# A transformer-block kernel with batched block-sorted attention: v mixed one batch ahead, loads reordered, matmuls in hand-set order

## The chip, the cores and the metric

The kernel runs on one core of one Trainium2 chip. The metric is the device time in microseconds (us) of one execution; lower is better. The engines are TensorE (PE), VectorE (DVE), ScalarE (ACT), GpSimd (POOL) and SyncE (SP, which here only issues transfers). Medians and 95% intervals are given. A run over 1.5% above the fastest of its kernel is called slow and is left out of every ratio.

A ratio is the mean time of one kernel's fast runs over the mean of the other's fast runs of the same rounds on the same chip. It is therefore not quite the ratio of the two medians that stand beside it.

## The reference

```python
# q, k, v: (4, 8, 768, 64); 8 blocks of 96 rows; w_tok (768,768), w_ch1 (512,2048), w_ch2 (2048,512)
P = sort_net                                  # (4, 8, 8, 8)
for _ in range(5):
    P = softmax over the last axis, then normalised over the one before it
k_sorted = einsum('bhij,bhjcd->bhicd', P, k_b)   # every block becomes a mix of 8 blocks
v_sorted = einsum('bhij,bhjcd->bhicd', P, v_b)
attn = softmax(scale * q_b @ k_sorted^T)         # inside each block of 96
x = (attn @ v_sorted), heads joined              # (4, 768, 512)
# then, per batch:
u   = x + lam * (w_tok @ (alpha1 * x + beta1))   # token mixing
out = u + lam * (relu((alpha2 * u + beta2) @ w_ch1) @ w_ch2)   # MLP over channels
```

Everything is held to a tolerance that the kernel meets with 16-bit operands.

## The kernel before

Each batch goes through: mixing v and k with P on TensorE, scores, exponentials on ACT, the value product, token mixing, and the two MLP matmuls ("hidden", tile `h_ps`, and "output", tile `ch_ps`). The MLP of batch b-1 is interleaved with the attention of batch b, so that TensorE always has wide matmuls to run while attention's small ones wait for ACT and DVE. ("Spins" are dummy matmuls, tile `spin_ps`, that the program runs early on while TensorE has nothing else.)

GpSimd issues the loads of q, k and v of the next batch (software queue). SP issues, in the order of its program, everything else (hardware queue; in r12 below the turns of q take SP from 79.05 to 88.43, and the next store is issued at 88.53): the turning of q (`qT<-qn`) and of the MLP input (`a2T<-u`) by DMA transposes, the stores, and the *regrouping* of mixed v, which goes out to memory (`vscr<-vA`) and comes back in another layout (`Vs<-vscr`, packets of 128 bytes).

```python
def load_raw(b, kv):                 # v or k of a batch, two transfers of 384 KB (batch 0 differs)
    ...
    for th in range(2):
        pool.dma_start(raw[th*64:(th+1)*64, :], src[b].rearrange(...)[th])

def cross_q(b):                      # q turned by six DMA transposes, issued by SP
    with tc.issue_after(regroup[b - 1].ins):
        for kt in range(NT):
            nc.sync.dma_start_transpose(qT_of[b][:, :, kt, :], ...)

def mix_v(b, banks=2, groups=range(6), copies=(...)):
    for n in groups[::banks]:
        vps = ...
        pe.matmul(vps[...], lhsT, raw[...], start=True, stop=True)
        copies[...](vA[...], vps[...])
    if groups[-1] < 5:
        return
    for th in range(2):              # regrouping: out ...
        nc.sync.dma_start(vscr[b, ...], vA[th*64:(th+1)*64, :, :])
    for par in range(2):             # ... and back
        regroup[b] = nc.sync.dma_start(Vs[b % NV][...], vscr[b]...)

def moe_ch(b, hf, kks=range(3)):     # output matmuls, residual, store
    ...
        ost = att.tile([128, C], FT, name="ost", tag="ost", bufs=2)
        ...
        dve.tensor_tensor(ost[:, lo:hi], cps[:], u_of[b][kt][:, lo:hi], ALU.add)
        nc.sync.dma_start(out[...], ost[0:96, lo:hi])

# ---- main order, from the end of batch 0's token mixing on (cut) ----
for n in range(6):
    moe_h(0, 0, range(5 + n, 6 + n))
    mix_v(1, 1, range(n, n + 1), (dve.tensor_copy,))
pool.tensor_copy(gate[:], Vs[1][0:1, 0, 0:2])   # the gate: GpSimd waits for batch 1's regrouped v
load_raw(2, 1)                                  # and only then loads v and k of batch 2
load_raw(2, 0)
...
pe.fixed = False                                # the scheduler orders the matmuls from here
for b in range(1, B):
    if b > 1:
        ...
        mixing_matrices(b)
        mix_v(b)                                # v of batch b mixed at the head of its own stage
        ...
        mix_k(b)
    emit_attention(b)
    ...                                         # MLP of batch b-1, token mixing of b
```

The *gate* is a tiny copy on GpSimd that reads the regrouped v of batch 1. Everything behind it in GpSimd's program, the loads of batch 2 above all, waits until that v has landed. `pe.fixed` says whether TensorE's instructions keep the program's order or the scheduler may move them.

The softmax here doesn't subtract the row's maximum and nothing guards it: scores larger than these inputs give would overflow.

## Time and profile before

| what | before |
|---|---|
| timed median of 3 runs | 269.09 us (268.78 to 269.38) |
| profiled span | 266.8 us |
| PE busy | 257.6 us, 97% |
| half clock on TensorE | none until the kernel's end |

The page of the kernel before, its first lines. The row of digits gives the busy tenths of PE in 40 equal slices; `PEclk` is the granted TensorE clock in tenths.

```profile
span 266.8 us, 5149 instructions
...
PE 257.6 (97%) x2049; PEld 141.6 (53%) x2059; DVE 154.8 (58%) x333; ACT 125.8 (47%) x232; POOL 92.5 (35%) x100
...
PE   7799999999999999999999999999999999999993
...
PEclk9999999999999999999999999999999999999999
...
PE 89%; ACT 4%; DVE 4%; issue 1%; DMA 1%; DVEq 0%; ACTq 0%
```

TensorE is the limit: it is never idle for a whole slice, and 89% of the chain that ended last is its own work. A gain has to come from TensorE's small gaps or from work taken off it.

The next lines are the timeline of PE in the kernel before: start, duration, engine, operation, tiles, count.

```profile
18.09 0.38 PE L65 MATMUL sc_ps<-qT,kT 64*96 64x96 f16 x8
...
42.64 2.60 PE L65 MATMUL h_ps<-a2T,W1p 128*128 128x384 bf16 x15
...
105.89 1.03 PE L65 MATMUL v_ps<-raw,bigV 128*128 128x512 f16 x4
107.59 0.59 PE L65 MATMUL v_ps<-raw,bigV 128*128 128x512 f16 x2
```

First scores start at 18.09, the first hidden matmul at 42.64, and v of batch 2 is mixed only at 105.89. GpSimd in the same kernel:

```profile
66.80 0.18 POOL L65 COPY gate<-Vs 1x2 f16<-1x2 f16 x1
66.92 1.08 POOL L65 DMA_DIRECT2D raw<-in_v_dram  x2
...
76.35 4.49 POOL L65 DMA_DIRECT2D qn<-in_q_dram  x5
```

The gate opens at 66.80 and v of batch 2 is issued at once, 39 us before TensorE wants it. Most of q comes after it. The next line is the view of the transfers of the kernel before, for those issued from 66 to 69 us: number, size of one, median us from issue to landing.

```profile
raw<-in_v_dram POOLq DMA_DIRECT2D x2, 384.0 KB, 8.4
```

So v of batch 2 lands near 76.

### The profile page before, as it was taken

What the parts mean: (1) busy time and instruction counts of PE and PEld (TensorE: products, weight loads), DVE (VectorE), ACT (ScalarE), POOL (GpSimd) and SP (SyncE); (2) the same over time, 40 slices, a digit from 0 to 9 for tenths busy, and PEclk for the clock granted to TensorE, in tenths of its full rate; (3) what the DMA queues carried; (4) which work ended last, traced back from release to release, by engine and by line L of the source; (5) the groups of instructions that cost most, each with busy time, mean ns of one, the idle gap of its engine ahead of it and who ended that gap; (6) DMA issues with size and microseconds to landing.
All of it is one profiled execution on the core that took longest, in us unless ns stands there. A gap on an engine that the chain in (4) does not pass through costs nothing.

```text
span 266.8 us, 5149 instructions
## 1 busy us (share of the span) xinstructions
PE 257.6 (97%) x2049; PEld 141.6 (53%) x2059; DVE 154.8 (58%) x333; ACT 125.8 (47%) x232; POOL 92.5 (35%) x100
## 2 busy tenths in 40 slices
PE   7799999999999999999999999999999999999993
PEld 2467745565565444554565444554565445545542
DVE  5878788629567966722585966704675962042033
ACT  3376757643585312980375404970474305504600
POOL 8524689203575615007917225002409000000000
PEclk9999999999999999999999999999999999999999
DMA  6999999999999544499996342494200432012012
GB/s 83 174 208 251 207 210 207 211 216 112 211 157 155 113 84 117 114 82 89 202 211 136 61 100 80 118 98 62 80 2 2 81 76 79 2 39 79 2 39 79
DMA packets 62423, 30.88 MB, mean 116 GB/s; under 512 B 48888, under 2 KB 58112, under 8 KB 62400
## 3 DMA queue, kind: packets, MB, share of 16 engines
q0 software_dynamic: 23024, 15.60, 39.4%
q1 hardware_dynamic: 39280, 14.89, 32.6%
q8 instruction: 16, 0.26, 0.4%
q14 instruction: 7, 0.06, 0.1%
q10 hardware_dynamic: 96, 0.07, 0.1%
HBM read 32.78 MB, written 8.65 MB: 155 GB/s over the span
## 4 chain that ended last, share of the span: by engine, by line
PE 89%; ACT 4%; DVE 4%; issue 1%; DMA 1%; DVEq 0%; ACTq 0%
PE ch_ps L65 31%; PE h_ps L65 30%; PE tok_ps L65 12%; PE x_ps L65 5%; PE sc_ps L65 4%; ACT kT L65 2%; PE v_ps L65 2%; PE k_ps L65 1%; PE q_ps L65 1%; ACT et L65 1%; DVE csum L65 1%; DVE P L65 1%; PE m_ps L65 1%; DVE rsum L65 1%; DMA P<-in_sort_net_dram 1%
## 5 line engine op out<-in xcount | busy, mean ns | idle before, releaser
L65 PE MATMUL h_ps<-a2T,W1p 128*128 128x384 bf16 x512 | 93.4, 326 | 0.1
L65 ACT ACTIVATE hTa<-h_ps 128x384 bf16<-128x384 f32 x96 | 45.9, 492 | 68.1 <-PE h_ps L65 67.0
L65 PE MATMUL ch_ps<-W2p,hTa 128*128 128x512 bf16 (+2 forms) x290 | 65.9, 370 | 0.5
L65 PEld LDWEIGHTS <-W1p 128*128 128x128 bf16 x512 | 47.5, 98 | 30.3 <-issue 0.9
L65 DVE TENSOR_TENSOR ch_ps<-ch_ps,lamB 128x512 f32<-128x512 f32 (+2 forms) x25 | 16.9, 676 | 63.2 <-PE ch_ps L65 60.5
L65 POOL TENSOR_SCALAR u<-b1lB,rs 128x512 f32<-128x512 f32 x18 | 28.8, 1610 | 64.1 <-DVE ost L65 59.3
L65 PEld LDWEIGHTS <-hTa 128*128 128x128 bf16 x300 | 28.7, 98 | 32.4
L65 PE MATMUL tok_ps<-x,w_tokT 128*128 128x512 f16 x144 | 32.1, 379 | 0.0
L65 POOL TENSOR_TENSOR u<-x,u 128x512 f32<-128x512 f16 x22 | 25.3, 1181 | 18.1 <-DVE x L65 17.3
L65 ACT ACTIVATE et<-sc_ps 96x768 f16<-96x768 f32 x32 | 24.9, 807 | 11.7 <-PE sc_ps L65 11.7
L65 ACT CAST u<-u 128x512 f16<-128x512 f32 x24 | 14.8, 618 | 24.8 <-DVE u L65 24.8
L65 PE MATMUL ch_ps<-W2p,hTb 128*128 128x512 bf16 (+2 forms) x100 | 25.0, 371 | 0.0
L65 PEld LDWEIGHTS <-w_tokT 128*128 128x128 f16 x180 | 14.8, 97 | 16.1
L65 DVE TENSOR_TENSOR tok_ps<-tok_ps,a1lB 128x512 f32<-128x512 f32 x24 | 16.5, 692 | 7.3 <-PE tok_ps L65 7.3
L65 DVE CAST kT<-k_ps 64x512 f16<-64x512 f32 x24 | 16.5, 688 | 3.4 <-PE k_ps L65 3.0
L65 DVE TENSOR_TENSOR x<-x_ps,recip 96x512 f16<-96x512 f32 (+2 forms) x32 | 17.6, 554 | 0.9
L65 DVE TENSOR_TENSOR u<-tok_ps,u 128x512 f32<-128x512 f32 x24 | 16.4, 688 | 1.7
L65 ACT ACTIVATE hTb<-h_ps 128x384 bf16<-128x384 f32 x32 | 15.3, 497 | 3.8 <-PE h_ps L65 3.4
L65 DVE TENSOR_TENSOR ost<-ch_ps,u 128x512 f32<-128x512 f32 (+2 forms) x25 | 16.6, 665 | 0.6
L65 POOL DMA_DIRECT2D qn<-in_q_dram x18 | 15.5, 875 | 4.2 <-PE q_ps L65 3.4
L65 PEld LDWEIGHTS <-hTb 128*128 128x128 bf16 x100 | 9.6, 98 | 10.9
L65 PEld LDWEIGHTS <-et 96*128 96x128 f16 (+2 forms) x288 | 12.4, 99 | 4.6 <-issue 1.2
(95 smaller groups left out, 214.7 us busy)
## 6 DMA issues: line engine op xcount, KB each, us to landing
out_dram<-ost SPq DMA_DIRECT2D x23, 192.0 KB, 2.2
raw<-in_v_dram POOLq DMA_DIRECT2D x8, 384.0 KB, 8.9
raw<-in_k_dram POOLq DMA_DIRECT2D x8, 384.0 KB, 10.9
vscr<-vA SPq DMA_DIRECT2D x6, 384.0 KB, 4.4
Vs<-vscr SPq DMA_DIRECT2D x6, 384.0 KB, 7.7
W1p<-in_moe_w_ch_dram POOLq DMA_DIRECT2D x4, 512.0 KB, 10.1
W2p<-in_moe_w_ch_dram POOLq DMA_DIRECT2D x4, 512.0 KB, 17.9
qn<-in_q_dram POOLq DMA_DIRECT2D x12, 128.0 KB, 5.8
```

The costliest lines, as they stand in the source:

```text
L65: ins = getattr(self.eng, name)(*args, **kwargs)
```

## The change

Intent: take switches between small and wide matmuls out of the attention stages, and start the first scores earlier. Its parts: (1) batch 0's k and v load by halves, k first; (2) the six copies that sort `w_tok` move from DVE to GpSimd; (3) v of batch 1 loads ahead of W1 and is mixed from the end of batch 0's attention on; W2 loads ahead of batch 2; (4) TensorE order is set by hand from batch 1 on: a `weave` of MLP matmuls with fewer, longer attention groups, and v of batch b+1 is mixed inside batch b's stage; (5) rows of u are made earlier, in 11 row buffers, from which results are stored directly (no `ost`).

```diff
@@ loads at the start @@
-    load_q(0)
-    load_raw(0, 1)
-    load_raw(0, 0)
+    load_q0(1)
+    load_raw0(0)          # k and v by halves, k first
+    load_raw0(1)
...
+    load_raw(1, 1)        # v of batch 1, ahead of W1
+    load_w1(range(2))
+    for n in range(3):
+        sort_wtok(n)      # now pool.tensor_copy
...
@@ end of batch 0 @@
+    mixes(1, 0)
     prep_rs()
...
+    load_q(1)
+    load_w2(range(4))     # all of W2 here: 40.8 us in the trace
+    tok_part(0, 0)
+    mixes(1, 1)
+    tok_part(0, 1)
+    mixes(1, 2)           # v of batch 1 regrouped from here on
...
@@ head of batch 1 @@
-    pool.tensor_copy(gate[:], Vs[1][0:1, 0, 0:2])
-    load_raw(2, 1)
-    load_raw(2, 0)
+    pool.tensor_copy(gate[32:64, :], Vs[1][32:64, 0, 0:2])
+    load_q(2)
+    load_raw(2, 1)
+    load_raw(2, 0)
+    cross_q(2, regroup[1])
+    moe_rows(1, range(5))
+    pe.fixed = True
@@ the loop over batches @@
-        if b > 1:
-            mixing_matrices(b)
-            mix_v(b)
-            mix_k(b)
-        emit_attention(b)
+        steps = ... attention_steps(b, ...)
+        if b < B - 1:
+            at = len(steps) - (3 if b == 1 else 6)
+            steps[at:at] = [(g, lambda n=n: mixes(b + 1, n)) for n, g in enumerate((1.2, 0.7, 1.1))]
+        weave(fill, steps)        # fill: MLP matmuls of batch b-1, in hand-set portions
+        run(fill)
@@ output @@
-            ost = att.tile([128, C], FT, name="ost", tag="ost", bufs=2)
+            u32 = u_of[(b, kt)]
-                nc.sync.dma_start(out[...], ost[0:96, lo:hi])
+                nc.sync.dma_start(out[...], u32[0:96, lo:hi])
```

(Cut to its core; names and lines are those of the change, arguments shortened where marked by dots.)

## The prediction

> **What bounds the kernel now.** TensorE. The page gives PE 257.6 us busy of a 266.8 us span (the timed median, 269.09, is 2.3 above the span), and the chain of waits is 89% PE. Busy time overcounts, so I took start-to-start times of matmuls from the timeline: 216 ns for 128x512, 162 for 128x384, about 30 for attention's small ones. The span then divides so (us):
> - 0 to 11.5: normalisation of the sort matrices, a DVE/ACT latency chain; PE only spins.
> - 11.5 to 34.0: batch 0's attention. Useful matmuls about 13.5, ten spins 2.2, nearly 7 of waits and switches. First scores at 18.1, because k loads last: its first half lands at 16.0 (issue plus landing time).
> - 34.0 to 42.6: token mixing, no gaps.
> - 42.6 to 262.4: gapless except 2.7 to 2.8 in each of three attention stages. There a change from wide matmuls to scores costs 0.12 and back 0.11, to k mixing 0.11; the rest is short waits.
> - End: 4.4 after the last matmul, unchanged.
>
> **What the change does, costed.**
> 1. Batch 0: k/v load by halves, k first; q turned during normalisation; ten spins out; uniform tail matmuls in the value product (mixed forms now cost about 0.09 a switch). First scores should come at about 14, and each head pair take about 2.9 of PE. Alone this would end the stage at about 28.5.
> 2. But w_tok lands at about 23 as before, and its sorting moves from DVE (six copies, 2.8 us) to GpSimd. [...] the trace shows only other operations there (1.2 and 1.6 us for 512). [...] v of batch 1, behind w_tok, lands at about 29.5. Row sums end at about 32 instead of 34.0: half of step 1's gain is eaten by arrivals.
> 3. v mixing of batch 1 (1.3 us of PE; ACT evicts at 1.0 each) moves in front of the first hidden matmul, which starts at about 41.4 instead of 42.6: gain about 2.5.
> 4. Attention of batches 1 to 3: eight attention groups instead of about fourteen, between hand-set stretches of MLP matmuls. [...] Gaps 2.7 to about 1.7 per batch: gain about 3.
> 5. Other matmul work is unchanged; DVE/ACT/GpSimd shifts are off the chain.
>
> Gain 5.5 to 6 in all.
>
> **Prediction.** 263.4 us, 8 in 10 between 260.0 and 267.5. Faster by over 2% (below 263.7): 0.52; within 2%: 0.45; slower: 0.03.
>
> **What would show it.** (1) first scores near 14; (2) PE waits for w_tok transposes between 24 and 31, released by GpSimd copies; (3) first hidden matmul at 40 to 43; (4) fewer, longer attention groups, gaps under 2 per batch; (5) last 47 us (MLP of batch 3) identical.
>
> **What would make it wrong.** GpSimd copies much quicker (then 261) or slower; loads of batch 2 colliding with W2 and the regrouping of batch 1's v: v of batch 2 is wanted near 71 and may land at 73 to 76, which in a fixed PE order stalls everything for 2 to 5; ACT, which takes more copies (gather, v mixing), falling behind between hidden-layer evictions and exponentials; the fixed order losing to the scheduler's.

The forecast's sum came to a span near 261 and a time of 263.4 us: a gain of 5.5 to 6, made of 2.5 for the first hidden matmul (point 3) and 3 for the gaps (point 4). The 32 for the row sums, and through it the 2.5 of point 3, contains the time of the sorting, as the author's estimate; the 3 of point 4 stands on the costs read from the trace.

## More of the kernel before

SP:

```profile
52.19 1.15 SPq L343 DMA_DIRECT2D vscr<-vA  x2
59.21 2.46 SPq L348 DMA_DIRECT2D Vs<-vscr  x2
...
83.10 7.17 SPq L149 DMA_TRANSPOSE qT<-qn  x5
90.37 8.90 SPq L601 DMA_TRANSPOSE a2T<-u  x6
...
109.26 1.10 SPq L343 DMA_DIRECT2D vscr<-vA  x2
```

SP never has two of these large jobs at one time: regrouping of batch 1 (52 to 61), turning of q (one transfer at 71, the other five from 83 to 90), turning of the MLP input (90 to 99), regrouping of batch 2 (from 109). That spacing looks like idle room. It is slack: time between a transfer's landing and its use.

## The result, and the profile after

| what | before (same chip) | after |
|---|---|---|
| timed median | 269.24 us (268.78 to 271.41), 4 runs | 280.00 us (278.65 to 281.05), 4 runs |
| ratio of the fast runs | | 1.038, 95% interval 1.031 to 1.046 |
| profiled span | 266.8 us | 276.9 us |
| half clock before the last 4 us | none | 13.65 us |

The change is slower by nearly 4%, where a gain of 2% was predicted. The page after:

```profile
span 276.9 us, 5127 instructions
...
PE 251.6 (91%) x2047; PEld 140.6 (51%) x2047; DVE 145.4 (53%) x317; ACT 136.2 (49%) x246; POOL 93.1 (34%) x100
...
PE   5988899999700999999999999999999999999994
...
PEclk9999999999965899999999999999999999999999
...
PE 76%; DMA 13%; POOL 6%; DVE 3%; issue 1%; ACT 1%; DVEq 0%; POOLq 0%
```

PE is busy 6 us less than before, yet the span is 10 longer. Two slices of the PE row read 0, and in the slices around them the granted clock falls. The whole loss is in one place. The timeline of PE after; the bracket gives the idle time just before the line and what ended it.

```profile
14.63 0.56 PE L65 MATMUL sc_ps<-qT,kT 64*96 64x96 f16 x16
...
42.34 2.88 PE L65 MATMUL h_ps<-a2T,W1p 128*128 128x384 bf16 x15
...
73.03 1.46 PE L65 MATMUL ch_ps<-W2p,hT 128*128 128x512 bf16 x6
89.84 1.01 PE L65 MATMUL v_ps<-raw,bigV 128*128 128x512 f16 x2 [15.35 <-DMA raw<-in_v_dram]
90.65 1.91 PE L65 MATMUL ch_ps<-W2p,hT 128*128 128x512 bf16 x4
```

The first scores come at 14.63 as predicted. Then TensorE stands still for 15.35 us because its next matmul in the fixed order mixes v of batch 2, and that v has not landed. The wait costs more than its own length: the windows on both sides of its end (length, then each engine's busy time, then PEclk, DMA share, GB/s) show a lower granted clock.

```profile
74.30:89.80 15.50, 0.19 (x1) 0.00 (x0) 0.50 (x2) 0.00 (x0) 7.73 (x5) 0.65 1.34 119
89.80:103.50 13.70, 13.66 (x98) 6.60 (x99) 6.99 (x15) 6.19 (x7) 1.56 (x1) 0.90 0.90 149
```

A mean of 0.90 over 13.7 us means 2.7 us at half clock after the restart, so about 1.4 us more. In that stretch the two v matmuls took 1.01 us where they take 0.59 at full clock. The clock record of this run shows half clock (0.50) for 13.65 us, from 78.9 to 92.5: it began about 4.4 us after TensorE had stopped, and ended 2.7 us after the restart. What sets its beginning and its length is not shown.

Why is v late? GpSimd after:

```profile
24.20 4.79 POOL L65 COPY wtp<-wt 128x1152 f16<-128x1152 f16 x6 [5.53 <-DMA wt<-in_moe_w_tok_dram]
...
40.78 2.99 POOL L65 DMA_DIRECT2D W2p<-in_moe_w_ch_dram  x4
66.30 0.18 POOL L65 COPY gate<-Vs 32x2 f16<-32x2 f16 x1 [22.53 <-DMA Vs<-vscr]
...
66.90 5.26 POOL L65 DMA_DIRECT2D qn<-in_q_dram  x6 [0.42 <-PE h_ps L65]
72.10 1.14 POOL L65 DMA_DIRECT2D raw<-in_v_dram  x2
```

and SP after:

```profile
47.61 11.32 SPq L364 DMA_DIRECT2D Vs<-vscr  x2
70.54 22.87 SPq L140 DMA_TRANSPOSE qT<-qn  x6
```

The view of the transfers after, for those issued from 72 to 73.2, and one line of the same view over the whole span, for all twelve DMA transposes of q:

```profile
raw<-in_v_dram POOLq DMA_DIRECT2D x2, 384.0 KB, 16.5
```

```profile
qT<-qn SPq DMA_TRANSPOSE x12, 8.3
```

Read together, three things push v of batch 2 from "landing near 76, wanted at 106" to "landing just before 89.8, wanted at 74".

1. The gate opens at 66.30, hardly earlier than before (66.80), although batch 1's v is mixed some 10 us earlier. (The two gates are not quite alike. The one before reads row 0, filled by the first of the two transfers that bring v back, and stood behind a load of q. The changed one reads rows 32 to 63, which need both. By the landing of the second transfer v is back at 66.15 instead of 68.42.) The regrouping reads back in 128-byte packets while W2 (issued at 40.78) arrives in 1 KB packets. In the records of the packets, the regrouping's queue and W2's move almost the same number of packets in each 2 us from 52 to 60: 386 and 385, 376 and 376, 382 and 381, 382 and 383. When W2 is in, regrouping alone moves 2,128 (62 to 64). What makes the counts equal is not shown. One record for one means an eighth of the bytes for the small ones: 0.05 MB in 2 us beside 0.38 MB of W2, where the regrouping alone moves 0.27 MB.
2. Behind the gate the six loads of q come first: 5.26 us of issue, and their 128-byte packets occupy the queue until about 75. v is issued at 72.10.
3. SP turns q meanwhile: of its 22.87 us it waits 11.8 for q to land, and its transposes fly beside the load of v. By the records of the packets, the loads of v and k together move 0.15 to 0.25 MB in each 2 us from 80 to 90; where almost nothing else flies (the kernel before, from 70 to 76) they move 0.35 to 0.37. Each suffers: the median turn takes 8.3 us to land, and v takes 16.5 us instead of 8.4.

### The profile page after: what moved, and what is told of

Read it like the earlier page. It is cut to its first block, busy times and chain, and to the rows that moved or that the text cites. A ratio compares the mean times of both kernels' runs of the same rounds, so it can differ in the third digit from the quotient of the medians.

```text
span 276.9 us, 5127 instructions
## 1 busy us (share of the span) xinstructions
PE 251.6 (91%) x2047; PEld 140.6 (51%) x2047; DVE 145.4 (53%) x317; ACT 136.2 (49%) x246; POOL 93.1 (34%) x100
## 4 chain that ended last, share of the span: by engine, by line
PE 76%; DMA 13%; POOL 6%; DVE 3%; issue 1%; ACT 1%; DVEq 0%; POOLq 0%
PE h_ps L65 29%; PE ch_ps L65 29%; PE tok_ps L65 9%; DMA wt<-in_moe_w_tok_dram 6%; DMA raw<-in_v_dram 6%; POOL qn L65 3%; PE sc_ps L65 2%; PE x_ps L65 2%; POOL wtp L65 2%; PE k_ps L65 1%; PE v_ps L65 1%; POOL raw L65 1%; DVE u L65 1%; PE q_ps L65 1%; DVE tok_ps L65 1%
## 5 line engine op out<-in xcount | busy, mean ns | idle before, releaser
L65 PE MATMUL h_ps<-a2T,W1p 128*128 128x384 bf16 x512 | 89.1, 326 | 0.1
L65 PE MATMUL ch_ps<-W2p,hT 128*128 128x512 bf16 (+2 forms) x400 | 88.4, 373 | 0.0
L65 ACT ACTIVATE hT<-h_ps 128x384 bf16<-128x384 f32 x128 | 60.4, 492 | 53.2 <-PE h_ps L65 52.7
L65 PEld LDWEIGHTS <-hT 128*128 128x128 bf16 x400 | 38.0, 99 | 42.1 <-issue 1.3
L65 DVE CAST kT<-k_ps 64x512 f16<-64x512 f32 x30 | 20.6, 687 | 3.9 <-PE k_ps L65 3.3
L65 DVE RECIPROCAL recip<-x_ps 96x8 f32<-96x8 f32 (+1 forms) x32 | 6.2, 195 | 27.5 <-PE x_ps L65 27.4
L65 ACT CAST vA<-v_ps 128x1024 f16<-128x1024 f32 x9 | 9.0, 1010 | 22.0 <-PE v_ps L65 22.0
L65 PE MATMUL v_ps<-raw,bigV 128*128 128x512 f16 x18 | 5.9, 410 | 15.3 <-DMA raw<-in_v_dram 15.3
L65 DVE TENSOR_TENSOR u<-ch_ps,u 128x512 f32<-128x512 f32 (+2 forms) x25 | 16.7, 667 | 0.8
L65 PEld LDWEIGHTS <-et 96*128 96x128 f16 (+1 forms) x288 | 12.0, 105 | 3.0 <-DVE x L65 0.6
```

The source lines that it names most:

```text
L65: ins = getattr(self.eng, name)(*args, **kwargs)
```

## The experiments

All kernels were built from the changed kernel ("after"). All outputs are right. Ratios are against the kernel before, on the same chip in the same rounds (medians of before lay from 268.58 to 269.24 us). "Wait" is the idle time of PE in the profile that names a transfer or an engine as its releaser.

| run | what it does | timed median, us | ratio (95%) | largest PE waits after 40 us |
|---|---|---|---|---|
| after | the change | 280.00 | 1.038 (1.031 to 1.046) | v of batch 2, 15.3 |
| e1_v_first | v, k ahead of q | 275.56 | 1.021 (1.014 to 1.028) | MLP input 3.7; 3.6 |
| e2_mix_after_tok | v mixed after token mixing | 283.27 | 1.050 (1.044 to 1.056) | row of u 8.7; 4.2; 2.8 |
| e3_no_gate | no gate | 272.72 | 1.013 (1.008 to 1.018) | MLP input 5.1; v 1.0 |
| e4_both | e1, v mixed at end of stage | 283.99 | 1.053 (1.045 to 1.062) | hidden 8.9; 4.7 |
| r5_defer_regroup | e1, regroup held back | 268.20 | 0.998 (0.995 to 1.001) | MLP input 3.6 |
| r6_all | r5, turning held, batch 3 gated | 275.08 | 1.024 (1.020 to 1.028) | v of batch 3, 9.4 |
| r8_defer_turn | only turning of q held back | 286.60 | 1.063 (1.057 to 1.069) | v of batch 3, 15.6; of 2, 6.1 |
| r9_cleared | r6, batch 3 loaded early | 269.94 | 1.005 (1.003 to 1.008) | regrouped v, 3.6 |
| r10_cleared_dve_sort | r9, sorts on DVE | 274.19 | 1.020 (1.018 to 1.021) | regrouped v, 4.7; (sort, 2.8) |
| r11_cleared_w2_gated | r9, W2 behind the gate | 271.66 | 1.010 (1.005 to 1.014) | 3.9; v of batch 2, 2.8 |
| r12_cleared2 | r5, batch 3 early, q of 3 gated | 272.27 | 1.010 (1.006 to 1.013) | row of u 6.1 |
| r14_rows12 | r12, 12 row buffers | 267.62 | 0.995 (0.991 to 1.000) | MLP input 3.2 |
| r15_split | write of v, turning, read | 264.68 | 0.983 (0.980 to 0.986) | MLP input, 1.4 at most |
| r16_split12 | r15, 12 row buffers | 265.43 | 0.986 (0.982 to 0.990) | 1.2 at most |

### First round: which part of the queue makes v late, and can it simply be wanted later?

**e1_v_first.** v and k of batch 2 go ahead of q.

```diff
-    load_q(2)
     load_raw(2, 1)
     load_raw(2, 0)
+    load_q(2)
     cross_q(2, regroup[1])
```

> Change with one edit: v and k of batch 2 are loaded ahead of q of batch 2 (all still behind the same gate). Theory (the loss is one wait of the fixed TensorE order for v of batch 2, which is late because q of batch 2 is loaded ahead of it): v lands about 10 us after its issue near 67, so at 76 to 78 instead of 89.7; the wait at its mixing (reached at 74) shrinks from 15.5 to 2 to 4 us, no half-clock stretch follows, time 264 to 267 us. Rival A (the hand-set order as such is slow, v is only where it shows): the wait moves elsewhere and the time stays above 274. Rival B (the gate alone makes it late): v still lands after 85, time above 274.

Measured: 275.56 us (272.09 to 277.05, one of four slow), ratio 1.021. The wait for v is gone:

```profile
74.73 0.59 PE L65 MATMUL v_ps<-raw,bigV 128*128 128x512 f16 x2
```

So the load order, with what flies beside it, is enough to remove the whole wait; the gate still opened at 66.08. But the gain expected did not come. (The profile is of the fastest run, with a mean clock of 0.991; the other three had 0.972 to 0.974, so they lost more to the lower clock than it shows.) New waits of 3.7 and 3.6 us stand before hidden matmuls, for the turned MLP input of batch 1 (released by DVE steps that themselves wait for the transposes). SP shows why:

```profile
93.26 2.56 SPq L364 DMA_DIRECT2D Vs<-vscr  x2
95.92 4.06 SPq L716 DMA_DIRECT2D out_dram<-u  x1
...
101.58 7.98 SPq L648 DMA_TRANSPOSE a2T<-u  x6
```

With v mixed on time, its regrouping (read back at 93.26) now runs ahead of the MLP-input transposes, and the stores behind it are held: the first takes 4.06 us to issue, and SP issues nothing else meanwhile. In the kernel before, v was mixed at 106, after the transposes (90 to 99).

**e2_mix_after_tok.** v of batch 2 is mixed after batch 1's token mixing, where the kernel before has it; loads unchanged.

```diff
-        if b < B - 1:
+        if 1 < b < B - 1:
             at = len(steps) - ...
...
+        if b == 1:
+            for n in range(3):
+                mixes(2, n)
         run(moe_ch(b - 1, 1, (1, 2)))
```

> Change with one edit: v of batch 2 is mixed after the token mixing of batch 1 (reached at about 96) instead of inside batch 1's attention (74); loads unchanged. Theory: v still lands near 90, nothing waits for it, the 15.5 us wait and about 1.5 us lost to the half clock behind it vanish: 260 us span, 261 to 263.5 timed, all other stages as in the change. Rival A (the fixed order is slow): other waits of over 5 us in total appear, time above 267.

Measured: 283.27 us, ratio 1.050: no faster than the change itself. Its profile fell on a slow run, so its waits are read for their places and releasers, not for a comparison of times. Token mixing waits 8.7 us for a row of u: GpSimd cannot make the row because its buffer is still being stored, and the stores stand behind the turning of q on SP (70.7 to 95.3). In the change as given the long wait for v hid that: the row came at 96.5 and token mixing began only at 105. A wait is not only cost; it also holds back everything behind it that would have collided.

**e3_no_gate.** The gate is dropped.

```diff
-    pool.tensor_copy(gate[32:64, :], Vs[1][32:64, 0, 0:2])
```

> Change without the gate that holds batch 2's loads until v of batch 1 is regrouped; order q, v, k kept. Theory (the wait for the gate, until 66.3, is the first half of v's lateness, q in front the second): v of batch 2 lands at 72 to 78; but the regrouping of v of batch 1 (128 B packets) now shares the DMA engines for longer and lands after 66, so a smaller wait at the first value product of batch 1 (reached at 67.3) appears. Time 264 to 270. Rival B (gate alone): time as without any wait, about 262. If the gate does not matter: above 274.

Measured: 272.72 us, ratio 1.013. q of batch 2 is issued at 59.06 and v at 64.26; the wait for v is 1.0 us at 76.37. So dropping the gate alone is worth about 7 us (ratio 1.013 against 1.038). Again the MLP input is late (5.1 us).

**e4_both.** e1 with v's mixing pushed to the end of the weave.

```diff
+            moved = steps[at:at + 3]
+            del steps[at:at + 3]
+            steps[at] = (1.9, steps[at][1])
+            steps += moved
```

> Change with v and k of batch 2 loaded ahead of q, and the three v mixings of batch 2 moved from the middle to the end of batch 1's attention weave (reached at about 81 instead of 74). Theory: v lands at 76 to 78, before it is wanted, no TensorE wait over 1 us after 43: 260 us span, 261 to 263 timed, about 2.5 to 3% under the kernel before. Rival A: above 267.

Measured: 283.99 us, ratio 1.053. The miss is large: hidden matmuls wait 4.7 us until 109.2 and 8.9 until 126.4. The view names ACT for the second, but behind ACT is DVE, which waits 12.0 us, until 122.0, for the last MLP-input transpose (issued at 107.92, landed at 121.89). The regrouping moved to 96, straight between the MLP-input transposes; the loads of batch 3 (issued 103 to 110) and the turning of its q (111 to 132) fly beside the last of them. Mixing v later is no repair while SP's order stays.

After this round the theory was: the lateness of v is one case of a more general thing. The new order has shortened the distance between every large transfer and its use, and SP's transfers now stand in the wrong order.

### Second round: the order on SP

**r5_defer_regroup.** e1, and the regrouping of v of batch 2 is held until the MLP-input transposes of batch 1 are issued.

```diff
-        if groups[-1] < 5:
+        if groups[-1] < 5 or b == 2:
             return
+        regroup_v(b)
...
         moe_a(b)
+        if b == 1:
+            with tc.issue_after(turned[-1].ins):
+                regroup_v(2)
```

> e1 (v and k of batch 2 ahead of q) and the regrouping of v of batch 2 (its two writes and two reads, 128 B packets) held until the transposing transfers of batch 1's MLP input have been issued. Second theory: in e1 the early mixing of v starts that regrouping at 93, in the same in-order SP queue and on the same DMA engines as those transposes, and so it is what made the first hidden matmul of batch 1 wait 3.9 us and DVE behind it. Expected: transposes issued near 92 instead of 101.6, both waits of 3.6 to 3.9 us in batch 1's hidden layer under 1 us, time 262 to 266. Rival C (the transposes are late for another reason, such as the loads of batch 3 or DVE order): the wait stays, time above 270.

Measured: 268.20 us, ratio 0.998. By the ratios that is 4 points, some 11 us, back from the change, and the wait before the first hidden matmul is gone, as the second theory had it. One wait of 3.6 us is left, before the second half of the MLP input.

**r6_all.** r5, the turning of q of batch 2 also held behind those transposes, and batch 3's loads behind a second gate on the regrouped v of batch 2.

```diff
-    cross_q(2, regroup[1])
...
         moe_a(b)
         if b == 1:
+            cross_q(2, turned[-1])
             with tc.issue_after(turned[-1].ins):
                 regroup_v(2)
...
         if b == 1:
+            pool.tensor_copy(gate[0:32, :], Vs[0][0:32, 0, 0:2])
-            load_q(3)
             load_raw(3, 1)
             load_raw(3, 0)
+            load_q(3)
-            cross_q(3, turned[-1])
...
         run(fill)
+        if b == 2:
+            cross_q(3, regroup[3])
```

> r5, and the transposing transfers of q of batch 2 also held until after those of batch 1's MLP input; the loads of batch 3 held behind a gate on the regrouped v of batch 2, v and k ahead of q; the q transposes of batch 3 behind the regrouping of v of batch 3. If all of the loss is collisions of transfers, no TensorE wait over 1 us is left after 43: span 259 to 262, timed 261 to 264, 2 to 3% under before. Rival A (the fixed TensorE order itself costs): above 267.

Measured: 275.08 us, ratio 1.024. The MLP input waits only 1.1 us now, but the second gate opens at 124.10, and v of batch 3 stalls TensorE for 9.4 us. A gate on a late transfer makes the next load late: the fault of batch 2, one batch on.

**r8_defer_turn.** The change with one edit: q of batch 2 is turned after batch 1's MLP-input transposes. Loads keep the change's order.

```diff
-    cross_q(2, regroup[1])
...
         moe_a(b)
+        if b == 1:
+            cross_q(2, turned[-1])
```

> Change with one edit: q of batch 2 is turned (transposing transfers) only after batch 1's MLP input, so these do not share the engines with the loads of v and k. If that sharing is a part of v's lateness [...], v lands at 79 to 82 instead of 89.7 and the wait at its mixing is 5 to 8 us, time 270 to 275; if only the order behind q counts, v lands after 87 and the time stays above 277.

Measured: 286.60 us, ratio 1.063. For the question asked it is clear. v is issued at 72.08, as in the change (72.10), with no turning beside it:

```profile
raw<-in_v_dram POOLq DMA_DIRECT2D x2, 384.0 KB, 7.2
```

It lands in 7.2 us instead of 16.5, and the wait falls from 15.3 to 6.1 us. So about 9 us of the wait comes from the turning of q beside the load, and the other 6 is the late issue behind q's loads. The time missed because q of batch 3 then waits for its buffer until q of batch 2 is turned (GpSimd waits 12.8 us), and v of batch 3, behind it, stalls TensorE for 15.6 us.

**r9_cleared.** r6 without the second gate: v and k of batch 3 are loaded right behind batch 2's loads and rows, q of batch 3 alone later.

```diff
     moe_rows(1, range(5))
+    load_raw(3, 1)
+    load_raw(3, 0)
     pe.fixed = True
...
         if b == 1:
-            pool.tensor_copy(gate[0:32, :], Vs[0][0:32, 0, 0:2])
-            load_raw(3, 1)
-            load_raw(3, 0)
             load_q(3)
```

> r6 with the loads of batch 3 set differently: v and k of batch 3 right behind batch 2's loads (their buffers are free from 57 on), q of batch 3 after batch 2's is turned; no second gate. In r6 v of batch 3 was held by that gate until 124 and TensorE waited 9.5 us for it at 121. Expected: v of batch 3 lands before 95, so that wait goes too and nothing over 1.3 us is left after 43: span 259 to 263, timed 261 to 265, 1.5 to 3% under before, with the TensorE order of the change untouched. Rival A (the fixed TensorE order costs): still above 267.

Measured: 269.94 us, ratio 1.005. All waits for loads are gone. One wait of 3.6 us is left, until 130.6, in the value product, for the regrouped v of batch 2. SP in this run:

```profile
92.19 10.65 SPq L652 DMA_TRANSPOSE a2T<-u  x6
102.94 7.79 SPq L140 DMA_TRANSPOSE qT<-qn  x6
110.77 1.23 SPq L363 DMA_DIRECT2D vscr<-vA  x2
...
117.33 8.14 SPq L368 DMA_DIRECT2D Vs<-vscr  x2
```

The read back can be issued only when the write has landed, 6.6 us after it was issued, and that wait for the landing stands at the end of the row: SP issues three stores in between, but none of its large jobs. This is the hint that r15 takes up.

### Third round: the other parts of the change, on the cleared version

**r10_cleared_dve_sort.** r9 with the sorting of `w_tok` back on DVE.

```diff
-            pool.tensor_copy(
+            dve.tensor_copy(
                 t_[:, :, :, lo:hi], ...
```

(and the three calls moved behind the scores loop of batch 0, so that DVE does not wait for `w_tok` in the middle of it)

> r9 with the six w_tok sorts back on VectorE, after the value products of head pair 2. They took 2.8 us there before, 4.8 us on GpSimd (24.2 to 29.0) in the change; w_tok itself lands at 24.2. If the GpSimd sorts hold the end of batch 0, the row sums end 1 to 2 us earlier than with r9 and the time falls by as much; if VectorE's own load there eats it (my expectation, weakly), it is within 0.5 us of r9.

Measured: 274.19 us, ratio 1.020, against 1.005 for r9; the intervals are far apart. TensorE waits 2.8 us for the DVE copies, until 30.2, the mean granted clock of the five runs is 0.971 to 0.981 (0.984 to 0.994 in r9), and the gate opens at 68.95 instead of 65.12. Against this placement of the DVE copies, sorting on GpSimd is a gain of about 4 us; the copies on DVE at their old place were not run in the new order.

**r11_cleared_w2_gated.** r9 with W2 loaded behind the gate.

```diff
     load_q(1)
-    load_w2(range(4))
...
     pool.tensor_copy(gate[32:64, :], Vs[1][32:64, 0, 0:2])
+    load_w2(range(4))
```

> r9 with W2 loaded behind the gate too, so that the regrouping of v of batch 1 does not share the DMA engines with W2. Theory: in the change it starts at 50 and gets one 128 B packet for each 1 KB packet of W2 until W2 ends at 60.5, and lands at 66, no earlier than in the kernel before although v was mixed 10 us earlier. Expected: the gate opens at 56 to 59 instead of 66.3; v of batch 2 then lands later or as late (W2 takes 10 us of the engines): time from equal to r9 to 5 us above it. Rival: the gate still opens after 64 (the regrouping is slow by itself).

Measured: 271.66 us, ratio 1.010. The gate opens at 58.11 instead of 65.12, so W2's packets did hold the regrouping of batch 1 back by 7 us. But W2 then stands before v of batch 2, which is waited for 2.8 us. The starvation is real, and removing it in this way gains nothing.

**r12_cleared2.** r5 with v and k of batch 3 early, and q of batch 3 loaded behind the regrouped v of batch 2.

```diff
     moe_rows(1, range(5))
+    load_raw(3, 1)
+    load_raw(3, 0)
...
         if b == 1:
+            pool.tensor_copy(gate[0:32, :], Vs[0][0:32, 0, 0:2])
             load_q(3)
-            load_raw(3, 1)
-            load_raw(3, 0)
-            cross_q(3, turned[-1])
...
         run(fill)
+        if b == 2:
+            cross_q(3, regroup[3])
```

> r5 (v, k of batch 2 ahead of q; v regrouping of batch 2 behind the MLP-input transposes of batch 1; q turned early as in r5) with v and k of batch 3 loaded right behind batch 2's loads, and q of batch 3 behind the regrouping of v of batch 2. In r9 the turning of q of batch 2 stood between the MLP transposes and the regrouping, which landed late for the first value product (3.8 us wait at 125, and a half-clock stretch behind it). Expected: regrouping lands before 122, no wait over 1.5 us after 43, clock 0.995 or more, span 260.5 to 263.5, timed 262.5 to 265.5: 1 to 2.5% under before. Rival A (the fixed order costs): still 267 or more without any long wait.

Measured: 272.27 us, ratio 1.010. Token mixing waits 6.1 us at 100.5 for the sixth row of u. GpSimd waited 10.9 us for that row's buffer: its store stood on SP behind the turning of q.

**r14_rows12.** r12 with 12 row buffers instead of 11 (room made by letting an identity matrix share one).

```diff
-            u_of[(b, kt)] = moep.tile([128, C], FT, name=f"u32_{kt}", tag="u32", bufs=11)
+            u_of[(b, kt)] = moep.tile([128, C], FT, name=f"u32_{kt}", tag="u32", bufs=12)
```

> r12 with twelve instead of eleven row buffers (the space is taken from the identity of the start). The change stores the result from the row buffer itself, so a row of batch 1 waits until a store of batch 0 has read its buffer; in r12 the stores stood in the in-order SP queue behind the turning of q of batch 2, the sixth row of batch 1 waited 10.9 us for one on GpSimd, and token mixing 6.1 us for that row. With a twelfth buffer no row of batch 1 waits for a store. Expected: token mixing of batch 1 without a wait over 0.5 us, MLP transposes of batch 1 begin near 94 instead of 101, no wait over 1.5 us after 43, clock 0.995 or more: span 260.5 to 263, timed 262.3 to 265, 1.3 to 2.5% under before. If the wait stays, the store was not its cause.

Measured: 267.62 us, ratio 0.995. That wait is gone, as expected; a wait for the MLP input (3.2 us at 109.3) is left, and with it a lower clock: the eight hidden matmuls behind the wait take 2.72 us (the eight behind r12's wait of 1.0 us take 1.46), and the mean granted clock of the profiled run is 0.993. (Two of the six runs had a mean clock of 1.000 and took 265.7 and 265.8 us.)

### Fourth round: is there a gain at all?

The repairs so far had each traded one wait for another, so this was still open: is the gain of the new matmul order real, or does the order need transfers at places where they cannot be?

**r15_split.** r9's order, but behind batch 1's MLP-input transposes SP issues first the write of v of batch 2, then the six turns of q, then the read back, so that the write lands under the turning. q of batch 3 is loaded behind the read back.

```diff
         moe_a(b)
         if b == 1:
-            cross_q(2, turned[-1])
             with tc.issue_after(turned[-1].ins):
-                regroup_v(2)
+                put_v(2)                       # vscr <- vA
+            cross_q(2, regroup[2])
+            with tc.issue_after(crossed[-1].ins):
+                get_v(2)                       # Vs <- vscr
...
+            pool.tensor_copy(gate[0:32, :], Vs[0][0:32, 0, 0:2])
             load_q(3)
```

> The run with the cleared queue, in which behind batch 1's MLP-input transposes SP issues first the write of v of batch 2 to memory, then the six turns of q of batch 2, then the read back; q of batch 3 loads only when that read has landed. First theory (the gain exists, and only collisions of transfers eat it): the read is issued near 111 instead of 117, lands near 121 to 123, the value product's wait for it falls from 3.6 to at most 1.3 us, no other PE wait is over 1.5, span 263 to 265.5, timed 264 to 266.5, ratio 0.983 to 0.992. Second theory (the new order needs its transfers where they cannot be, so a repair only moves the wait): the wait comes back somewhere else (scores for q, or the hidden layer for the MLP input) with 3 us or more, and the timed median stays at 268 to 271.

Measured: 264.68 us (263.47 to 264.99, 6 runs), ratio 0.983, 95% interval 0.980 to 0.986: the first version that is clearly under the kernel before. Its page and SP:

```profile
span 263.2 us, 5127 instructions
...
PEclk9999999999999999999999999999999999999999
```

```profile
92.15 10.98 SPq L658 DMA_TRANSPOSE a2T<-u  x6
103.19 1.22 SPq L367 DMA_DIRECT2D vscr<-vA  x2
104.51 9.68 SPq L142 DMA_TRANSPOSE qT<-qn  x6
114.28 2.54 SPq L374 DMA_DIRECT2D Vs<-vscr  x2
```

The read goes out at 114.28 instead of 117.33 and takes 2.54 us to issue. Its PE waits:

```profile
PE h_ps L65 <- DVE u L65: 2.6, 2, 1.4
PE k_ps L65 <- DMA raw<-in_k_dram: 0.3, 1, 0.3
```

and its turns of q, in the view of the transfers:

```profile
qT<-qn SPq DMA_TRANSPOSE x12, 2.5
```

A turn lands in 2.5 us (8.3 in the change). No transfer holds TensorE directly for more than 0.3 us. What is left is twice the MLP input (the view names the DVE step before it), 1.4 us at most each time, and the clock stays full to the end (mean 1.000). The first theory (the gain exists, and only collisions of transfers eat it) holds here, with the span, 263.2, and the time inside what it expected.

**r16_split12.** The same with 12 row buffers.

```diff
-            u_of[(b, kt)] = moep.tile([128, C], FT, name=f"u32_{kt}", tag="u32", bufs=11)
+            u_of[(b, kt)] = moep.tile([128, C], FT, name=f"u32_{kt}", tag="u32", bufs=12)
```

> The same with 12 row buffers instead of 11. First theory: if rows are not what is waited for any more, within 1 us of the run with 11; if they are (a PE wait in token mixing for u in the run with 11), this one is faster by that wait, and ends at 262.5 to 265.5. Second theory: 268 to 271, like the run with 11.

Measured: 265.43 us, ratio 0.986. The intervals of the two overlap, so the twelfth buffer is worth nothing here; rows are no longer what is waited for. The second theory (268 to 271) falls for both runs.

Not run: a version in which the scheduler orders TensorE's instructions from batch 1 on. Whether hand-setting in itself gains anything is left open.

## Why the prediction was wrong

The prediction's sum was a span near 261 and a time of 263.4. Where possible each term is compared with start-to-start times of matmuls in the two traces.

- **"First scores should come at about 14."** Right: 14.63, and 18.09 before.
- **The sorting of `w_tok` on GpSimd.** Measured: six copies in 4.79 us, 1.6 per pair, done at 29.0. What was missed is the worth of it: on DVE, behind the scores, the sorts cost 4 us more (r10). Token mixing, which follows the row sums, starts at 33.0 (34.0 before), where the prediction had them end at about 32: 1 us of step 1's gain is left, not 2.
- **"First hidden matmul at about 41.4 instead of 42.6: gain about 2.5"** (with v's mixing, 1.3, out of the way). It starts at 42.34, so the term is 1.6 us: 0.3 for the start plus the 1.3 of mixing. It is 2.0 in r15.
- **"Gaps 2.7 to about 1.7 per batch: gain about 3."** Too small. In batches 2 and 3 only about 0.7 us of gaps each is left, of 3.0 before. From the first hidden matmul to the last matmul, TensorE's excess over start-to-start work falls from about 8.9 us to about 3.9, the long wait and the half clock left out: a gain of about 5.0. The switch, about 0.1 us in the trace (0.09 from a hidden matmul to scores, 0.11 back), was costed about right. The waits among small groups, which fewer groups also remove, were not.
- **"Other matmul work is unchanged"; "last 47 us (MLP of batch 3) identical".** Right: from the first hidden matmul of the last MLP to the end the spans have 45.7 us before and 45.6 after.
- **"DVE/ACT/GpSimd shifts are off the chain."** Wrong: in the chain that ended last, transfers have 13% and GpSimd 6% after; GpSimd was not in it before.
- **The step that failed: "v of batch 2 is wanted near 71 and may land at 73 to 76, which in a fixed PE order stalls everything for 2 to 5".** It was named as a risk and left out of the sum. v was wanted at 74 and landed just before 89.8, the stall was 15.35 us, and the half clock behind it cost about 1.4 us more. The term is mis-sized for three reasons that the runs separate: the gate did not open earlier although v was mixed earlier, because W2's packets starve the regrouping (with W2 behind the gate it opens 7 us earlier, r11); v stands behind q's loads (about 6 us of the wait, r8); and it flies beside the turning of q (about 9 us: 16.5 to land instead of 7.2, r8).
- **"Slower: 0.03."** That chance was far too small for the same reason. It took a stall of 5 us for the worst, while nothing in the profile bounded it. The transfers in the kernel before looked fast because 39 us of slack and an otherwise quiet queue lay around them. With that slack removed, their position in the queues is what counts.

The sum with measured terms, with 0.2 for a shorter tail after the last matmul: 266.8 - 0.3 - 1.3 - 5.0 - 0.2 + 15.4 + 1.4 = 276.8, and the span is 276.9. For r15: first hidden matmul at 41.96 (0.7 earlier), 1.3 of mixing, 4.4 of gaps, 0.2 of tail, and 2.9 given back in two waits for the MLP input (start-to-start): 266.8 - 0.7 - 1.3 - 4.4 - 0.2 + 2.9 = 263.1, and the span is 263.2. (The gap terms are what is left of these very spans, so the sums close by construction; they divide the time and prove nothing more.) Most of the predicted gain was real, 1.7% in r15 where 2% was predicted; it was lost to contention among transfers, and most of it comes back when SP's and GpSimd's transfers are put into the order of their use.

What stays open: how the 15.35 us divide exactly, since the three causes overlap (e1 alone and e3 alone each remove almost all of the wait for v), and why the MLP input is still waited for twice in r15.

## What to carry to other kernels

When work is moved earlier in a fixed matmul order, list each transfer it needs with its issue, its landing and the time it is now wanted, and give the missing slack a number in the sum, not in the risks. Here SP's transfers of unrelated kinds waited for one another (in r12 GpSimd waited 10.9 us for a store that stood behind the turning of q): put such transfers in order of use, let one's landing be covered by the issue of the next, and look in the records for small packets beside large ones (here 0.05 MB in 2 us instead of 0.27) and for transposes beside loads (here 16.5 us to land instead of 7.2). If a repair only moves the wait, read the next queue's order before giving the idea up: here several orders of the transfers had to be put right together before the gain showed.
